# TensorE's program begins with leaps to two of its later points, and its loop is no longer put on a block edge

## The chip, the cores and the metric

The kernel runs on one core of a Trainium2 chip. A core has five engines with programs of their own (TensorE or PE, VectorE or DVE, ScalarE or ACT, GpSimd or POOL, SyncE or SP), which meet only at semaphores, and 16 DMA engines that carry data between main memory (HBM) and the on-chip memory, and the engines' own program code as well. The metric is device time in microseconds (us): lower is better.

## The reference

A decoding step for two batch entries (B = 2, one new position, D = 576) mixes an attention block with a dense block, by a gate:

```python
g = sigmoid((x * gate_w).sum(-1, keepdims=True))
q = (x @ wq).reshape(B, 1, H, Dh)            # H = 32 heads of Dh = 128
p = softmax(einsum("bhqd,bhkd->bhqk", q, k_cache) * Dh**-0.5)
a = einsum("bhqk,bhkd->bhqd", p, v_cache).reshape(B, 1, H * Dh) @ wo
b = gelu(x @ w1 + b1) @ w2 + b2              # F = 4608
return g * a + (1 - g) * b
```

All is float32. `k_cache` and `v_cache` have 4096 positions for each of 64 (batch, head) pairs, 134 MB each; the weights `wq`, `wo`, `w1`, `w2` are some 10 MB each. Everything is read once.

## The kernel before

**Data.** One large on-chip tile, `ring`, has three slots. `wq` and `w1` fill it first. The 64 heads are then taken in N = 16 quads of four (`E = 4`): quad i's K goes into slot i % 2, its V into slot 2 (the last V into slot 0). `w2` and `wo` follow into slots that come free. All large loads are issued by SyncE, in program order, so each waits there until its slot is released; the small ones (`b1`, the two rows of `x`, `gate_w`, `b2`) are issued by ScalarE.

**Before the quads.** TensorE's first work is `turn_x` (L318), which turns `x` and `gate_w` and needs the small loads; then come the gate, the projection with `wq`, the gathering of q, and the projection with `w1`. The first K load is issued when TensorE has read `wq`, the second when it has read `w1` (`load_k`, L474).

**A quad.** `scores(i)` (L517) multiplies K by q on VectorE and adds up over Dh, in part on GpSimd. `max_t` (TensorE) and `max_n` (VectorE) find the maximum, `softmax` (ScalarE) makes p. `attend` (L558) is 32 f32 matrix products on TensorE, p times V. `keep` (VectorE) and `combine` (TensorE) add the result to the accumulator.

**After the quads.** TensorE multiplies the 36 rows of `w2` into an accumulator (`acc_mm`), then rows 0 to 22 of `wo` (`FOLD = 23`). Rows 23 to 31 are done in four column parts each (`part`, L699), the last row's parts as their data lands; two copies and a store of 4.5 KB end the kernel.

**How the order is written.** The engines' programs are not in the order of the Python text but in lists: every call of `pe`, `dve`, ... appends an `Op` with its engine and what it reads and writes; `Flow.plan` works out the waits, and `Flow.write` (L91) writes each engine's list out. Operations marked `loop=(name, turn, place, slot)` are written once, as the body of a hardware loop (`nc.Fori`) with one register for the turn, whose waits are computed from the register. Only TensorE has such a loop: 15 turns of `attend`, `max_t`, `combine`. The last entry of the mark, 0, goes to `head_slot`: the loop's first instruction is loaded at slot 0 of a code block, the unit in which an engine's program is fetched, and a branch jumps over the padding ahead of it.

Of the kernel before, what the change touches and what calls it, by code (L numbers as in the profile page):

```python
# [27 lines left out]
class Flow:  # L28
# [12 lines left out]
    def op(self, engine, fn, r=(), w=(), a=(), dma=None, loop=None):  # L41
# [18 lines left out]
        self.ops.append(o)  # L60
        return o

    def plan(self):
        for o in self.ops:
            for d in o.deps:
                d.needed = True
        turns = {}
        for o in self.ops:
            if o.loop:
                turns.setdefault((o.loop[0], o.loop[2]), []).append(o)  # L70
        for same in turns.values():
            if any(o.needed for o in same):
                for o in same:
                    o.needed = True
        count, known = {}, {e: {} for e in ENGINES}
        for o in self.ops:
            k = known[o.engine]
            for d in sorted(o.deps, key=lambda d: -d.number):
                sem, v = d.done
                if k.get(sem, 0) < v:  # L80
                    o.waits[sem] = max(o.waits.get(sem, 0), v)
                    for s, n in d.knows.items():
                        k[s] = max(k.get(s, 0), n)
            sem = o.dma or o.engine
            count[sem] = count.get(sem, 0) + (16 if o.dma else 1 if o.needed else 0)
            o.done = sem, count[sem]
            o.knows = {**k, sem: max(k.get(sem, 0), count[sem])}
        self.count = count
        return turns

    def write(self):  # L91
        nc, turns = self.nc, self.plan()
        sems = {s: self.issued.get(s) or nc.alloc_semaphore(f"s_{s}") for s in self.count}
        for e in ("sp", "act", "pool", "dve", "pe"):
            at = self.at[e]
            ops = [o for o in self.ops if o.engine == e and o.dma not in self.issued]
            while ops:
                if not ops[0].loop:
                    self.emit(at, sems, ops.pop(0), None)
                    continue  # L100
                name, slot = ops[0].loop[0], ops[0].loop[3]
                body = [turns[k] for k in sorted(k for k in turns if k[0] == name)]
                assert ops[:len(body)] == [same[0] for same in body]
                ops = [o for o in ops if not o.loop or o.loop[0] != name]
                n = len(body[0])
                with nc.Fori(0, n, 1, engines=[at.engine], head_slot={at.engine: slot}) as i:
                    for same in body:
                        step = {}
                        for sem in {s for o in same[1:] for s in o.waits}:
                            v = [o.waits[sem] for o in same[1:]]  # L110
                            by = v[1] - v[0]
                            assert all(z - y == by for y, z in zip(v, v[1:])) and v[0] - by > 0
                            assert same[0].waits.get(sem, 0) <= v[0] - by
                            step[sem] = v[0] - by, by
                        assert set(same[0].waits) <= set(step)
                        self.emit(at, sems, same[0], (i, step))
        return sems

    def emit(self, at, sems, o, turn):
        if turn:  # L120
            for s, (base, by) in sorted(turn[1].items()):
                at.wait_ge(sems[s], turn[0] * by + base)
        else:
            for s, v in sorted(o.waits.items()):
                at.wait_ge(sems[s], v)
        i = o.fn()
        if o.dma:
            i.then_inc(sems[o.dma], 16)
        elif o.needed:
            i.then_inc(sems[o.engine], 1)  # L130
# [3 lines left out]
def kernel(  # L134
# [14 lines left out]
    nc = tc.nc  # L149
# [81 lines left out]
    with tc.tile_critical() as section:  # L231
        f = Flow(nc, {"first": first})
# [10 lines left out]
        def pe(fn, r=(), w=(), a=(), loop=None):  # L243
            return f.op("pe", fn, r, w, a, loop=loop)
# [9 lines left out]
        def mm(o, lhsT, rhs, start, stop):  # L254
            return ten.matmul(o, lhsT, rhs, start=start, stop=stop, skip_group_check=True)  # L255


        at = 0
        wts = {}
        for name, w in (("wq", wq), ("w1", w1)):  # L260
            n = w.shape[1]
# [162 lines left out]
        def half_mm(lhsT, rhs, k, s, start=False):  # L424
            o = 64 * (k % 2) + 32 * s
            return mm(acc[o:o + lhsT.shape[-1]], lhsT, rhs, start, False)

        def acc_mm(lhsT, rhs, k, start=False):
            for s in range(NS):
                i = half_mm(lhsT, rhs[:, s * DS:(s + 1) * DS], k, s, start)  # L430
            return i
# [32 lines left out]
        def slot(k):  # L464
            return ring[:, k * SLOT:(k + 1) * SLOT]
# [5 lines left out]
        def rows_of(t):  # L471
            return t.rearrange("p (r d) -> p r d", d=DH)
# [59 lines left out]
        def max_t(i, loop=None):  # L532
            pe(lambda: mm(mt, mxt.to_broadcast([P, P]), ident, True, True), r=["mxt", "ident"], w=["bank2"], loop=loop)

        def max_n(i):
            s = i % 2
            dve(
                lambda: vec.tensor_reduce(bs[s], mt.rearrange("o (e p) -> o e p", e=E), AX.X, ALU.max, negate=True),  # L538
                r=["bank2"], w=[f"bs{s}"],
            )  # L540

        def softmax(i):
            s = i % 2
            p = p_all[:, :NT * EB].rearrange("p (t c) -> p t c", c=EB)

            def fn():
                for e in range(E):
                    w = slice(e * PE_, (e + 1) * PE_)
                    ins = sca.activation(  # L549
                        p[w, :, e * RB:(e + 1) * RB], st[s][w].rearrange("p (t c) -> p t c", c=RB), AF.Exp,  # L550
                        bias=bs[s][w, e:e + 1], accum_out=rs[w, i * E + e:i * E + e + 1],
                    )
                return ins

            act(fn, r=[f"st{s}", f"bs{s}"], w=["p"], a=["rs"])
            act(lambda: sca.copy(now, pick[:, NO - E - i * E:2 * NO - E - i * E]), r=["pick"], w=["now"])

        def attend(i, name, loop=None):  # L558
            v = rows_of(slot(2 if name == "slot2" else 0))

            def fn():
                for t in range(NT):
                    j = t % 4
                    ins = mm(
                        av[32 * j:32 * j + 32], p_all[:, EB * t:EB * t + 32],
                        v[:, RB * t:RB * (t + 1)].rearrange("p r d -> p (r d)"), t < 4, t >= NT - 4,
                    )
                return ins

            pe(fn, r=["p", name], w=["bank4"], loop=loop)  # L570
# [8 lines left out]
        def combine(i, loop=None):  # L579
            pe(  # L580
                lambda: mm(oall, now, avs.rearrange("p r d -> p (r d)"), False, False),
                r=["now", "avs"], a=["bank1"], loop=loop,
            )

        for i in range(N):
            k = i - 1
            if i:
                max_n(k)
                softmax(k)
            scores(i)  # L590
            if i:
                attend(k, "slot2", loop=("quads", k, 0, 0))
                load_v(i)
            if i + 2 < N:
                load_k(i + 2)
            s = i % 2
            dve(lambda s=s: vec.tensor_reduce(mxt, st[s], AX.X, ALU.max), r=[f"st{s}"], w=["mxt"])  # L597
            max_t(i, loop=("quads", k, 1, 0) if i else None)
            if i:
                keep(k)  # L600
                combine(k, loop=("quads", k, 2, 0))


        srcs = {"w2": w2.rearrange("(p r) n -> p (r n)", r=NF), "wo": wo.rearrange("(p r) n -> p (r n)", r=32)}
# [12 lines left out]
        k = N - 1  # L617
# [8 lines left out]
        o = load_rows(2 * SLOT, "w2", 0, 14)  # L626
        o = load_rows(o, "w2", 14, 28)
        release(1)
        o = load_rows(SLOT, "w2", 28, NF)
        o = load_rows(o, "wo", 0, 9)  # L630
        o = load_rows(o, "wo", 9, 16)
# [3 lines left out]
        o = 0  # L635
        for a, z in ((16, 23), (23, 27), (27, 30), (30, 31)):
            o = load_rows(o, "wo", a, z)
        for a, z in ((0, DS), (DS, DS + DO), (DS + DO, D)):
            o = load_rows(o, "wo", 31, 32, (31 * D + a, 31 * D + z))
# [15 lines left out]
        turn = late(P)  # L655
# [18 lines left out]
        ops = bank[6][:, :NO]  # L674
# [13 lines left out]
        for r in range(NF):  # L688
            t, name = row("w2", r)
            pe(lambda t=t, r=r: acc_mm(hg[:, r], t, r), r=["hg", name], a=["bank0"])  # L690
        for r in range(FOLD):
            t, name = row("wo", r)
            pe(lambda t=t, r=r: acc_mm(oP[:, :, r], t, r), r=["oP", name], a=["bank0"])
# [34 lines left out]
        sems = f.write()  # L728
# [33 lines left out]
```

## Time and profile before

| | |
|---|---|
| median of 3 runs | 720.75 us (720.68 to 720.82) |
| profiled execution, time | 720.49 us |
| profiled execution, span from first to last instruction | 718.7 us |
| mean granted TensorE clock | 0.656 |
| busy: PE / DVE / ACT / POOL | 239.1 / 518.2 / 41.6 / 144.2 us |
| DMA | 308.71 MB, mean 430 GB/s |

The time of a run takes in a little before the first and after the last instruction, so the profiled execution's own time is 1.8 us more than its span. Times in the profile's rows count from the span's start. "Busy" is time in which an engine executed something; an idle engine matters only if it is what the end waits for. Queue q1 is SyncE's data queue, q10 ScalarE's; "instruction" queues carry program code.

### The profile page before, as it was taken

The page shows a single profiled execution, that of the slowest core. Times are in us where ns is not written, and L with a number is a line of the kernel's source. Part 1 is how long each engine was busy: PE and PEld are TensorE (multiplying, and loading weights), DVE is VectorE, ACT ScalarE, POOL GpSimd, SP SyncE. Part 2 cuts the span into 40 slices and gives each one's busy share as a digit, 9 for nine tenths or more (in the row PEclk, how much of TensorE's full clock was granted, in tenths as well). Part 3 has the DMA queues.
Part 4 walks back from the last instruction along what each step waited for, and adds up shares of the span by engine and source line. Part 5 has one row for each costly group of instructions (what it writes and reads, how often), then busy time and mean ns, then how long its engine had stood idle before and what let it go on. Part 6 is the DMA issues. An engine that isn't in the chain of part 4 may idle for free.

```text
span 718.7 us, 3903 instructions
## 1 busy us (share of the span) xinstructions
PE 239.1 (33%) x1659; PEld 68.5 (10%) x1659; DVE 518.2 (72%) x150; ACT 41.6 (6%) x157; POOL 144.2 (20%) x28
## 2 busy tenths in 40 slices
PE   0684004151514033140505060504123140506566
PEld 0221001010101000010101010101000010101122
DVE  0103999999969696969697896969696969698100
ACT  0020010101010101010101000010101010101000
POOL 1020133140404040311304040404040221304000
PEclk9977557565656657565757565666656575756788
DMA  9999999999999999999999999999999999999997
GB/s 411 409 428 450 419 453 419 445 430 430 434 427 445 423 445 430 434 441 423 438 423 452 423 441 434 430 441 419 445 423 449 427 441 434 427 441 423 420 428 322
DMA packets 7076, 308.71 MB, mean 430 GB/s; under 512 B 782, under 2 KB 1166, under 8 KB 1436
## 3 DMA queue, kind: packets, MB, share of 16 engines
q1 hardware_dynamic: 7044, 308.55, 99.3%
q8 instruction: 6, 0.10, 0.0%
q10 hardware_dynamic: 24, 0.05, 0.0%
q14 instruction: 2, 0.02, 0.0%
HBM read 308.59 MB, written 0.00 MB: 429 GB/s over the span
## 4 chain that ended last, share of the span: by engine, by line
DMA 56%; DVE 38%; PE 4%; POOL 0%; issue 0%; ACTq 0%; ACT 0%; POOLq 0%; DVEq 0%
DMA ring<-in_A_k_cache_dram 43%; DVE ring L521 22%; DVE st L526 11%; DMA ring<-in_A_v_cache_dram 6%; DVE st L528 5%; DMA ring<-in_A_wo_dram 4%; PE bank L255 4%; DMA ring<-in_gate_w_dram 3%; POOL ring L275 0%; PE bank L320 0%; DVE mxt L597 0%; DVE bs L538 0%; ACTq L250 0%; POOL ring L369 0%; DVE ring L313 0%
## 5 line engine op out<-in xcount | busy, mean ns | idle before, releaser
L521 DVE TENSOR_TENSOR ring<-ring,q_all 128x16384 f32<-128x16384 f32 x16 | 275.6, 17224 | 85.0 <-DMA ring<-in_A_k_cache_dram 85.0
L255 PE MATMUL bank<-ring,p_all 128*32 128x512 f32 x1024 | 146.5, 736 | 343.6 <-DMA ring<-in_A_v_cache_dram 343.6
L525 POOL TENSOR_TENSOR ring<-ring 128x3968 f32<-128x3968 f32 x16 | 138.0, 8624 | 473.1 <-DVE ring L521 473.1
L526 DVE TENSOR_REDUCE st<-ring 128x66 f32<-128x8448 f32 x16 | 143.2, 8953 | 0.6
L255 PEld LDWEIGHTS bank<-ring,p_all 128*32 128x32 f32 x1024 | 35.9, 132 | 458.9 <-DMA ring<-in_A_v_cache_dram 355.9
L528 DVE TENSOR_REDUCE st<-ring 128x62 f32<-128x3968 f32 x16 | 68.6, 4286 | 0.6
L549 ACT ACTIVATE p_all<-st,bs 32x128 f32<-32x128 f32 x64 | 25.5, 398 | 561.3 <-DVE bs L538 560.7
L255 PE MATMUL bank<-ring 128*32 128x384 f32 (+8 forms) x410 | 48.0, 526 | 11.2 <-DMA ring<-in_A_wo_dram 7.5
L255 PE MATMUL bank<-ident,mxt 128*128 128x128 f32 x32 | 9.2, 376 | 92.5 <-DVE mxt L597 92.5
L491 DVE TENSOR_TENSOR ring<-bank,ring 128x384 f32<-128x384 f32 x3 | 1.5, 553 | 32.6 <-PE bank L255 32.6
L724 DVE COPY ring<-bank 2x144 f32<-2x144 f32 x2 | 0.6, 300 | 33.3 <-PE bank L255 33.2
L255 PE MATMUL bank<-avs,now 128*64 128x512 f32 x32 | 23.5, 826 | 2.1 <-DVE avs L574 0.9
L574 DVE TENSOR_TENSOR avs<-bank,selr 128x512 f32<-128x512 f32 x16 | 10.9, 681 | 15.7 <-PE bank L255 15.7
L255 PEld LDWEIGHTS bank<-ring 128*32 128x32 f32 (+5 forms) x410 | 17.9, 122 | 40.8 <-issue 24.7
L255 PEld LDWEIGHTS bank<-ident,mxt 128*128 128x128 f32 x32 | 5.6, 220 | 106.8 <-DVE mxt L597 106.8
L313 DVE COPY ring<-ring 3x64 f32<-3x64 f32 x2 | 0.3, 181 | 19.4 <-DMA ring<-in_gate_w_dram 19.4
L255 PE MATMUL bank<-ring,hg 128*2 128x288 f32 x144 | 11.0, 462 | 2.6 <-DMA ring<-in_B_w_dram 2.6
L549 ACT ACTIVATION_READ_ACCUMULATOR p_all<-st,bs 32x1 f32 x64 | 11.8, 184 | 0.0
L408 POOL TENSOR_TENSOR ring<-ring 64x512 f32<-64x512 f32 x4 | 4.0, 1038 | 37.5 <-ACT ring L386 37.5
L320 PE MATMUL bank<-ident,ring 3*128 3x3 f32 x6 | 0.8, 254 | 23.8 <-DVE ring L313 23.8
L538 DVE TENSOR_REDUCE bs<-bank 128x4 f32<-128x128 f32 x16 | 4.7, 291 | 1.9 <-PE bank L255 1.9
L597 DVE TENSOR_REDUCE mxt<-st 128x1 f32<-128x128 f32 x16 | 4.6, 286 | 0.6
(65 smaller groups left out, 33.8 us busy)
## 6 DMA issues: line engine op xcount, KB each, us to landing
ring<-in_B_w_dram SPq DMA_DIRECT2D x1, 9216.0 KB, 46.2
ring<-in_B_w_dram SPq DMA_DIRECT2D x2, 4032.0 KB, 23.9
ring<-in_A_wo_dram SPq DMA_DIRECT2D x2, 2016.0 KB, 37.3
ring<-in_A_wo_dram SPq DMA_DIRECT2D x1, 2592.0 KB, 38.6
ring<-in_B_w_dram SPq DMA_DIRECT2D x1, 2304.0 KB, 32.8
ring<-in_B_w_dram SPq DMA_DIRECT2D x1, 1152.0 KB, 48.4
ring<-in_A_wo_dram SPq DMA_DIRECT2D x1, 1152.0 KB, 34.1
ring<-in_A_wq_dram SPq DMA_DIRECT2D x1, 1024.0 KB, 24.3
```

Of the source, the lines that this page charges most:

```text
L255: return ten.matmul(o, lhsT, rhs, start=start, stop=stop, skip_group_check=True)
L320: i = ten.transpose(xps[:, c, :B + 1], s, ident[:B + 1, :B + 1])
L408: lambda t=t, u=u: gps.tensor_mul(t, qall.unsqueeze(1).to_broadcast([NO, NQ, DH]), mine[:, u:u + NQ].unsqueeze(2).to_broadcast([NO, NQ, DH ...
L491: lambda m=m, b=b: vec.tensor_add(hrow[:, m * FC:(m + 1) * FC], bank[b][:, :FC], b1r[:, m * FC:(m + 1) * FC]), r=[f"bank{b}", "b1r"], a=[" ...
L521: lambda: vec.tensor_mul(kt, kt, q.unsqueeze(1).to_broadcast([P, R, DH])),
L525: pool(lambda: gps.tensor_add(h[:, :, :DH2], h[:, :, :DH2], h[:, :, DH2:]), r=[name], a=[name + "h"])
L526: dve(lambda: vec.tensor_reduce(st[s][:, HALVED:], kt[:, HALVED:], AX.X, ALU.add), r=[name], w=[f"st{s}"])
L528: lambda: vec.tensor_reduce(st[s][:, :HALVED], h[:, :, :DH2], AX.X, ALU.add),
L538: lambda: vec.tensor_reduce(bs[s], mt.rearrange("o (e p) -> o e p", e=E), AX.X, ALU.max, negate=True),
L549: ins = sca.activation(p[w, :, e * RB:(e + 1) * RB], st[s][w].rearrange("p (t c) -> p t c", c=RB), AF.Exp, bias=bs[s][w, e:e + 1], accum_o ...
L574: lambda: vec.tensor_mul(avs, av.rearrange("p (r d) -> p r d", d=DH), selr.unsqueeze(2).to_broadcast([P, RB, DH])), r=["bank4", "selr"], w ...
L597: dve(lambda s=s: vec.tensor_reduce(mxt, st[s], AX.X, ALU.max), r=[f"st{s}"], w=["mxt"])
```

## The change

`Flow` gets a method `stone`, which appends an operation without a function: a mark in an engine's list. TensorE's list gets two such marks: one ahead of its part of the first quad (ahead of `max_t(0)` and of the loop), and one behind the `w2` rows, ahead of the `wo` rows. Where an engine has marks, `write` now begins its program with a loop of two passes. In the first, with the register `turn` at 0, the compare-and-branch at each mark skips the work in front of the next one: the program branches to the first mark, from there to the second, sets `turn` to 1 and goes back to the start. In the second pass the work between the marks is done in order. What comes after the second mark follows the loop. The inner loop of 15 turns is no longer given a slot of a code block: it is loaded where it falls. The writing of one operation or loop moves into a method of its own, `next`, unchanged but for `head_slot`. The other engines' programs have no marks and stay as they are.

```diff
+    def stone(self, engine):
+        self.op(engine, None)
...
             ops = [o for o in self.ops if o.engine == e and o.dma not in self.issued]
+            stones = sum(o.fn is None for o in ops)
+            if stones:
+                turn = nc.alloc_registers(f"{e}_turn", engines=[at.engine])
+                nc.regs_mov(turn, 0)
+                with nc.Fori(0, 2, 1, engines=[at.engine]):
+                    for k in range(stones):
+                        work, stone = f"{e}_work{k}", f"{e}_stone{k}"
+                        nc.br_cmp(turn, 1, on_true=work, on_false=stone, comp_op="IS_EQ", engines=[at.engine])
+                        with nc.body(work, valid_engines=[at.engine]):
+                            while ops[0].fn:
+                                self.next(at, sems, ops, turns)
+                            ops.pop(0)
+                            nc.br(stone, engines=[at.engine])
+                        nc.switch_body(stone, valid_engines=[at.engine])
+                    nc.regs_mov(turn, 1)
             while ops:
...
+                self.next(at, sems, ops, turns)
         return sems
+
+    def next(self, at, sems, ops, turns):
...
-                with nc.Fori(0, n, 1, engines=[at.engine], head_slot={at.engine: slot}) as i:
+        with nc.Fori(0, n, 1, engines=[at.engine]) as i:
...
         for i in range(N):
             k = i - 1
+            if i == 0:
+                f.stone("pe")
             if i:
                 max_n(k)
                 softmax(k)
             scores(i)
             if i:
-                attend(k, "slot2", loop=("quads", k, 0, 0))
+                attend(k, "slot2", loop=("quads", k, 0))
...
             pe(lambda t=t, r=r: acc_mm(hg[:, r], t, r), r=["hg", name], a=["bank0"])
+        f.stone("pe")
         for r in range(FOLD):
             t, name = row("wo", r)
```

More of the change, by code (lines that the diff above doesn't have):

```diff
@@ L96, in write @@
             ops = [o for o in self.ops if o.engine == e and o.dma not in self.issued]
-            while ops:
[L98 to L105, printed above, removed]
-                with nc.Fori(0, n, 1, engines=[at.engine], head_slot={at.engine: slot}) as i:
[L107 to L116, printed above, removed]
@@ new lines, in write @@
+            while ops:
+                self.next(at, sems, ops, turns)
+        return sems
+    def next(self, at, sems, ops, turns):
+        nc = self.nc
+        if not ops[0].loop:
+            self.emit(at, sems, ops.pop(0), None)
+            return
+        name = ops[0].loop[0]
+        body = [turns[k] for k in sorted(k for k in turns if k[0] == name)]
+        assert ops[:len(body)] == [same[0] for same in body]
+        ops[:] = [o for o in ops if not o.loop or o.loop[0] != name]
+        n = len(body[0])
+        with nc.Fori(0, n, 1, engines=[at.engine]) as i:
+            for same in body:
+                step = {}
+                for sem in {s for o in same[1:] for s in o.waits}:
+                    v = [o.waits[sem] for o in same[1:]]
+                    by = v[1] - v[0]
+                    assert all(z - y == by for y, z in zip(v, v[1:])) and v[0] - by > 0
+                    assert same[0].waits.get(sem, 0) <= v[0] - by
+                    step[sem] = v[0] - by, by
+                assert set(same[0].waits) <= set(step)
+                self.emit(at, sems, same[0], (i, step))
@@ L597 @@
             dve(lambda s=s: vec.tensor_reduce(mxt, st[s], AX.X, ALU.max), r=[f"st{s}"], w=["mxt"])
-            max_t(i, loop=("quads", k, 1, 0) if i else None)
+            max_t(i, loop=("quads", k, 1) if i else None)
             if i:
                 keep(k)
-                combine(k, loop=("quads", k, 2, 0))
+                combine(k, loop=("quads", k, 2))
         srcs = {"w2": w2.rearrange("(p r) n -> p (r n)", r=NF), "wo": wo.rearrange("(p r) n -> p (r n)", r=32)}
```

## The prediction

> **What bounds the kernel now.** I read the page's DMA rows first, because the GB/s row of the slices is flat.
>
> ```profile
> span 718.7 us, 3903 instructions
> ...
> PE 239.1 (33%) x1659; PEld 68.5 (10%) x1659; DVE 518.2 (72%) x150; ACT 41.6 (6%) x157; POOL 144.2 (20%) x28
> ...
> q1 hardware_dynamic: 7044, 308.55, 99.3%
> q8 instruction: 6, 0.10, 0.0%
> ...
> q14 instruction: 2, 0.02, 0.0%
> ```
>
> TensorE is busy a third of the span, VectorE 72%; the 16 DMA engines carry ring traffic for 99.3%. The span is bytes over rate, plus a short end. The same rows hold what the change is about: queue q8 moved six packets of code, 0.10 MB, so 16 KB each. Asked window by window, the DMA view shows where they lie, 37:39, 60.5:62.5, 106.5:108.5, 676.5:678.5, 693:695 and 712.9:714.9, and one each; the first and last are shown, and between them the stretch 110:670, with no q8 row at all.
>
> ```profile
> q1 hardware_dynamic: 23, 0.85, 99.8%
> q8 instruction: 1, 0.02, 3.0%
> ...
> q1 hardware_dynamic: 4187, 242.73, 100.0%
> q14 instruction: 2, 0.02, 0.0%
> ...
> q1 hardware_dynamic: 461, 0.57, 79.2%
> q8 instruction: 1, 0.02, 3.0%
> ```
>
> A share of 3.0% of 16 engines over 2 us is 0.03 x 16 x 2 = 0.96 us of one engine: that is what one block of code costs the transfers. None is fetched in 110:670, where the loop turns. After the loop there are three. TensorE executes 2 x 1659 = 3318 matrix instructions; by the code 504 lie ahead of the loop (each f32 product is two weight loads and two matmuls) and a turn has 136, 2040 in 15 turns, which leaves 774 behind it. 774 over three fetches is one per 258: code is fetched block by block, as the program advances. So q8 is TensorE's.
>
> Next, does TensorE ever stand still for code? The chain of waits, first the start and then the end:
>
> ```profile
> 1.48 1.06 POOL ring L275
> ...
> 4.29 18.98 DMA ring<-in_gate_w_dram
> ...
> 23.80 0.86 PE bank L320 x6
> ...
> 24.99 10.94 PE bank L255 x74
> ...
> 35.94 34.24 DMA ring<-in_A_k_cache_dram
> ...
> 622.34 46.68 DMA ring<-in_A_v_cache_dram
> ...
> 669.15 8.58 PE bank L255 x64
> ...
> 677.75 31.71 DMA ring<-in_A_wo_dram
> ...
> 709.51 6.76 PE bank L255 x106
> ...
> 716.29 0.27 ACT ring L724
> ```
>
> Up to 23.80 TensorE waits for `gate_w`, the last of four small loads on ScalarE's queue. At the end it starts on wo rows 16 and up at 709.51. The 6.76 us that follow look like TensorE's, but the timeline's weight loads say that it catches up with the last rows as they land:
>
> ```profile
> 713.14 0.83 PEld L255 LDWEIGHTS bank<-ring 128*2 128x2 f32 x26 [0.34 <-issue]
> ...
> 715.21 0.11 PEld L255 LDWEIGHTS bank<-ring 128*2 128x2 f32 x8 [0.26 <-DMA ring<-in_A_wo_dram]
> 715.47 0.46 PEld L255 LDWEIGHTS bank<-ring 128*2 128x2 f32 x8 [0.15 <-DMA ring<-in_A_wo_dram]
> ```
>
> The last parts of row 31 wait for DMA (0.26, then 0.15 us). Around the fetch near 713.2 the idle ahead of the weight loads is 0.34 us, the beat of the rows before it: TensorE was not stopped by code there. So what ends the kernel is the last landing, plus one matmul, a copy and the store.
>
> **The change part by part.** (1) The walk. TensorE sets a register, enters a loop of two passes, and on the first pass branches to the first stone (ahead of the first `max_t`), from there to the second (behind the w2 rows), and back; on the second pass it works. A handful of register and branch instructions, at tenths of a us, before 23.80. The real price is that each leap lands in code not fetched yet. The trace has no missed branch, so I bound it. Below: 0.96 us, the packet alone. Above: 18.98 us, `gate_w` from issue to landing. Nearest to a block asked for while the engines are full of 64 KB rows is a step of ScalarE's queue:
>
> ```profile
> 2.57 1.10 ACTq L250 DMA_DIRECT2D ring<-in_B_b_dram  x1
> ...
> 4.29 0.29 ACTq L250 DMA_DIRECT2D ring<-in_gate_w_dram  x1
> ...
> 23.46 0.29 DVE L313 COPY ring<-ring 3x64 f32<-3x64 f32 x2 [19.36 <-DMA ring<-in_gate_w_dram]
> ```
>
> Four loads from 2.57 to 23.27 (4.29 + 18.98) are 5.2 us each; I take that. Two misses from about 1.5 us, where the engines begin (the chain's first row), end at 11.9, three (if the way back misses too) at 17.1. Both are before 23.80, so the cost on the path is 0. With the upper bound two misses would end at 39.5, 15.7 us late. How much lateness is free?
>
> ```profile
> 35.94 25.05 SPq L250 DMA_DIRECT2D ring<-in_A_k_cache_dram  x2
> ...
> 49.12 0.28 PEld L255 LDWEIGHTS bank<-ring 1*64 1x64 f32 x2 [0.92 <-issue]
> ...
> 51.02 0.20 PEld L255 LDWEIGHTS bank<-ring 128*32 128x32 f32 x8 [1.61 <-issue]
> ```
>
> SyncE issues the first K load at 35.94, when TensorE is done with wq, and the second at about 60.7 (the row's end, 35.94 + 25.05, less the 0.3 of one issue), when it is done with w1. The first K load lands at 35.94 + 34.24 = 70.18, so the second is queued 9.5 us before the engines need it; allow 2 for its start. TensorE also waits 1.61 us for w1's last rows at 51.02. So some 9 us of lateness, to 33, cost nothing; DMA runs dry only beyond that. The first K load has more room (it queues behind w1, whose rows are still arriving near 51).
>
> (2) Which fetches remain. If the blocks stay where they are put, each leap brings its target, and if the next block comes along as it does in straight running, four blocks arrive before 23.80; the straight run then asks for one more or none. Four or five fetches for six: the padding that put the loop on a block is gone too. The engines are full everywhere, so a fetch moved to the start costs its engine the same 0.96 us there. What counts is which of the 16 finishes last:
>
> ```profile
> 714.00:714.10 0.10, 0.10 (x12) 0.09 (x2) 0.00 (x0) 0.00 (x0) 0.00 (x0) 1.00 0.81 282
> ...
> 714.60:714.70 0.10, 0.10 (x14) 0.10 (x6) 0.00 (x0) 0.00 (x0) 0.00 (x0) 1.00 0.54 173
> ...
> 715.00:715.10 0.10, 0.10 (x10) 0.00 (x0) 0.00 (x0) 0.00 (x0) 0.00 (x0) 1.00 0.48 150
> ...
> 715.20:715.30 0.10, 0.10 (x8) 0.10 (x8) 0.00 (x0) 0.00 (x0) 0.00 (x0) 1.00 0.28 86
> ...
> 715.40:715.50 0.10, 0.10 (x10) 0.03 (x4) 0.00 (x0) 0.00 (x0) 0.00 (x0) 1.00 0.01 0
> ```
>
> The next to last column is the share of DMA engines busy. They drain over 1.5 us: 0.48 x 16, about eight, are still at work at 715.05, four or five at 715.25, none at 715.45. Three fetches fall behind 670, so at most three of these eight are late for that; if all three were freed, others would end at about 715.25. Gain 0.1 to 0.2 us; I take 0.15. Bounds: were every late engine brought to the middle of the drain (714.65) it would be 0.8 us; and if two of the early fetches meet on one of the late engines, it ends 0.96 us later than now.
>
> (3) The loop not aligned. 504 instructions and some ten waits and branches precede it; by 258 to a block, its 143 (136 and seven of waits and counting) begin near the start of the third block, shifted by whatever is loaded ahead of it, which the trace doesn't show. It lies inside a block unless that is over some 100 slots. Inside, or with both blocks kept, a turn costs as now: 0. In each turn TensorE waits for V, by the page's costliest matmul group, so tenths of a us more per turn are covered:
>
> ```profile
> L255 PE MATMUL bank<-ring,p_all 128*32 128x512 f32 x1024 | 146.5, 736 | 343.6 <-DMA ring<-in_A_v_cache_dram 343.6
> ```
>
> 343.6 us of idle over 16 turns is 21 us a turn.
>
> (4) Stone two behind the w2 rows: a branch, a move, an add and a compare ahead of wo row 0. TensorE waits there for data: 0.
>
> Sum against the profiled execution, 720.49 (span 718.7 and 1.8 around it): 0 + 0 + 0 + 0 - 0.15 = 720.35. The median of the runs is 720.75, 0.26 above that execution, so 720.6.
>
> [...]
>
> **The rivals.** *1, slower: blocks are not kept, and the loop straddles an edge.* Then the walk is lost (its fetches are repeated in the straight run), and each of 14 ways back finds its first block replaced by the one prefetched behind the loop. Two to three fetches a turn are 28 to 42 x 0.96 = 27 to 40 us of engine time, 1.7 to 2.5 us on each of 16: 722.4 to 723.3. It decides from two fetches a turn. For it: nothing shows a second block kept. Against: 143 instructions straddle only with a long preamble; I give the straddle one in four, two blocks one in three. Blocks not kept but no straddle: about 11 fetches in place of six, spread on more engines, 720.5 to 721.3, no change by the bound. Chance of rival 1: 0.08, with a walk so long that DMA runs dry (39.5 - 33 = 6.5 us, 727) in another 0.01.
>
> *2, faster: code fetches cost more than I see.* If the wait at 709.51 were late through q8 and not through wo's own bytes, and the drain were even, the gain would be the 0.8 us of the upper bound plus 0.96 of the fetch near 713.2, 1.7 us: 719.0. Against it: the ring is at 100.0% without any q8 in 110:670, and one fetch holds one engine in 16. 0.03.
>
> *3, the change does not do what it says:* the way back drops what was fetched, the six fetches come again where they were. Then the walk's fetches lie beside them: 720.7 to 721.2; its chance, 0.2, is part of "no change".
>
> **How the numbers follow.** Main case 0.68 (720.6; own range 720.3 to 721.2), rival 3 and its kin 0.2, rival 1 0.09, rival 2 0.03. Differences under 0.2% (1.44 us) are what I call the same: 0.88. Slower 0.09, faster 0.03. The range runs from half of the 0.8 us bound, 720.2, to a doubly charged late engine and a little of rival 1, 721.7.
>
> **What would show it.** Right: q8 packets before 24 us, four or so, and at most one behind 670; `gate_w` and first matmul still near 23.8; K loads issued near 35.9 and 60.7; none in 110:670; last landing of wo within 0.3 us of now. Wrong: q8 packets in the loop (rival 1), first matmul beyond 33, idle of "issue" ahead of TensorE in the last 10 us.

## The result, and the profile after

The changed kernel takes 723.42 us (median of 7 runs, 722.46 to 723.58), the kernel before 720.64 us in runs beside them: a ratio of 1.0035 (95% interval 1.0025 to 1.0044), 2.8 us slower. The seven runs lie in two clumps, three near 722.5 and four near 723.5. No change was forecast (720.6, range 720.2 to 721.7).

The page, and then the DMA view of the windows 0:20, 20:30, 110:670, 670:700 and 700:722 (the code queue's rows; for 110:670 all rows):

```profile
span 721.8 us, 3914 instructions
...
q1 hardware_dynamic: 7044, 308.55, 98.9%
q8 instruction: 10, 0.16, 0.1%
...
q8 instruction: 3, 0.05, 1.6%
...
q8 instruction: 2, 0.03, 1.9%
...
q1 hardware_dynamic: 4184, 242.80, 100.0%
q14 instruction: 2, 0.02, 0.0%
...
q8 instruction: 2, 0.03, 0.4%
...
q8 instruction: 1, 0.02, 0.3%
```

Ten blocks of code instead of six: five ahead of 30 us, two more by 110, none while the loop turns, and three behind it. The leaps brought five, and the straight run fetched its five all the same. The chain of waits, the start and the end:

```profile
4.28 18.99 DMA ring<-in_gate_w_dram
...
23.80 0.86 PE bank L344 x6
...
37.31 34.66 DMA ring<-in_A_k_cache_dram
...
680.05 32.58 DMA ring<-in_A_wo_dram
...
712.67 6.71 PE bank L279 x106
...
719.41 0.28 ACT ring L751
```

TensorE starts at 23.80, as before. The first K load, whose start moved (37.31 for 35.94) but which waits behind `w1` in either kernel, lands at 71.97 instead of 70.18: 1.8 us of the loss is there in the first 72 us. At the end wo rows 16 and up are in at 712.63 instead of 709.46. What the DMA engines do in the last microseconds, from the windows view (the next to last column is the share of the 16 engines at work; 0.06 is one of them):

```profile
715.00:715.10 0.10, 0.10 (x8) 0.07 (x2) 0.00 (x0) 0.00 (x0) 0.00 (x0) 0.50 0.46 167
716.00:716.10 0.10, 0.10 (x6) 0.03 (x2) 0.00 (x0) 0.00 (x0) 0.00 (x0) 1.00 0.33 127
717.00:717.10 0.10, 0.10 (x12) 0.08 (x8) 0.00 (x0) 0.00 (x0) 0.00 (x0) 1.00 0.06 23
718.00:718.10 0.10, 0.10 (x13) 0.05 (x4) 0.00 (x0) 0.00 (x0) 0.00 (x0) 1.00 0.06 23
718.40:718.50 0.10, 0.10 (x8) 0.00 (x0) 0.00 (x0) 0.00 (x0) 0.00 (x0) 1.00 0.07 23
```

Before, none was at work at 715.45. Now one engine alone, with fifteen idle, works on from 717 to past 718.4. The kernel waits for it. The totals hide this: bytes, rate and the busy times of the engines are nearly as before (308.78 MB at 428 GB/s, TensorE busy for 238.8 us, VectorE for 518.2).

### The profile page after: what moved, and what is told of

It is laid out like the page before. It is cut to its first block, busy times and chain, and to the rows that moved or that the text cites. A ratio compares the mean times of both kernels' runs of the same rounds, so it can differ in the third digit from the quotient of the medians.

```text
span 721.8 us, 3914 instructions
## 1 busy us (share of the span) xinstructions
PE 238.8 (33%) x1659; PEld 68.4 (9%) x1659; DVE 518.2 (72%) x150; ACT 41.6 (6%) x157; POOL 144.2 (20%) x28
## 2 busy tenths in 40 slices
DMA packets 7080, 308.78 MB, mean 428 GB/s; under 512 B 782, under 2 KB 1166, under 8 KB 1436
## 3 DMA queue, kind: packets, MB, share of 16 engines
q1 hardware_dynamic: 7044, 308.55, 98.9%
## 4 chain that ended last, share of the span: by engine, by line
DMA 56%; DVE 38%; PE 4%; POOL 0%; issue 0%; ACTq 0%; ACT 0%; POOLq 0%; DVEq 0%
DMA ring<-in_A_k_cache_dram 43%; DVE ring L545 21%; DVE st L550 11%; DMA ring<-in_A_v_cache_dram 6%; DVE st L552 5%; DMA ring<-in_A_wo_dram 5%; PE bank L279 4%; DMA ring<-in_gate_w_dram 3%; POOL ring L299 0%; PE bank L344 0%; DVE mxt L623 0%; DVE bs L562 0%; ACTq L274 0%; POOL ring L393 0%; DVE ring L337 0%
## 5 line engine op out<-in xcount | busy, mean ns | idle before, releaser
L279 PEld LDWEIGHTS bank<-ring 128*32 128x32 f32 (+5 forms) x410 | 17.6, 121 | 41.6 <-issue 21.8
```

## The experiments

Two theories were put to the test. *Pile*: the leaps' fetches come on top of the straight run's; each holds one DMA engine (for 0.96 us, by its packet), which would never catch up if each large load, which lands in 16 parts, gave every engine a fixed share; the end would be set by the engine that got most. *Layout*: the shifted blocks, or the loop that is not on a block edge, cost it.

**Leaps and layout apart.** Both marks removed, the loop still unaligned:

```diff
-            if i == 0:
-                f.stone("pe")
...
-        f.stone("pe")
```

> The changed kernel without its two marks: no leaps, only the loop left where it falls. Pile theory (the leaps' own fetches come on top of the six of the straight run, and the DMA engine that got most of them ends last): q8 has 5 packets, last wo landing within 0.3 us of the kernel before, 720.3 to 720.9. Rival, layout (the shifted blocks move the straight run's fetches onto engines that are late, or the loop pays for its place): 722.4 to 723.6 as with the change.

The leaps with the loop back on slot 0:

```diff
-        with nc.Fori(0, n, 1, engines=[at.engine]) as i:
+        with nc.Fori(0, n, 1, engines=[at.engine], head_slot={at.engine: 0}) as i:
```

> The leaps with the loop put back on slot 0 of a block. Pile theory: still about ten to eleven q8 packets, five of them before 24 us, and 722.3 to 724. Layout rival: back to 720.3 to 720.9.

The two marks moved into the first block (and taken out where they were):

```diff
         pe(turn_x, r=["xg", "xe", "ident"], w=["bank2"])
+        f.stone("pe")
...
         pe(gate, r=["gT", "xT"], w=["bank7"])
+        f.stone("pe")
```

> The same two marks, but the first behind turn_x and the second behind the gate product, some 30 instructions into the program: the walk stays in the first block and fetches nothing. Pile theory: 5 q8 packets, both leaps under 0.5 us, 720.3 to 720.9. Rival (the two-pass loop and its branches cost something by themselves): over 721.5.

Measured: without leaps 720.47 us (ratio 1.0000, 0.9991 to 1.0009; five q8 packets); aligned leaps 723.65 (1.0044, 1.0030 to 1.0057; eleven packets); near leaps 720.49 (0.9999, 0.9990 to 1.0008; five packets). The code queue's rows, without leaps and with aligned leaps:

```profile
q8 instruction: 5, 0.08, 0.0%
```

```profile
q8 instruction: 11, 0.18, 0.1%
```

The layout theory falls: the unaligned loop costs nothing (720.47), and saves a fetch that nobody misses (five packets for six, ten for eleven). The two-pass loop and its branches cost nothing either (720.49). The line view of the compare-and-branch shows the leaps, of the near ones and then of the changed kernel (durations in ns: least, median, longest):

```profile
L109 PEldq COMPARE_BRANCH  x4: 71/138/217, 1.7 to 23.8; - x4
```

```profile
L109 PEldq COMPARE_BRANCH  x4: 71/4132/9097, 1.7 to 59.5; - x4
```

In the trace the two far leaps take 8.2 and 9.1 us, the near ones 0.2: TensorE stands at the branch until a block is in (the packet of the first leap's fetch ends at 8.5 us, the leap at 9.9). The walk, way back included, ends at 19.8 us, ahead of 23.80.

**One leap instead of two.** Only the first mark, or only the second (the other `f.stone("pe")` removed).

> Only the first mark (ahead of max_t(0)): one leap out and back. Pile theory: two or three fetches before 24 us, of which two coincide, then the straight run's five; the latest DMA engine ends some 3 us behind the first at the first K load (3.5 with the change, 1.7 before), and 721.8 to 723.3. If the cost grew evenly with the number of extra fetches, three of five would give 722.3; if it takes both leaps to make a pair of fetches at once, 720.6 to 721.5.

> Only the second mark (behind the w2 rows): one leap out and back, further. [...]

Measured: 721.98 (1.0020, 1.0011 to 1.0029) and 721.92 (1.0020, 1.0010 to 1.0029). Half the loss each, at either distance; but the halves do not add up leap by leap, as the section on the sum below shows. Three fetches come early in each: one near 7.6 and two at once near 15.

**The pair.** Two fetches at once looked worse than one: by the trace's packets a fetch alone takes 0.9 to 1.1 us, one of a pair 1.5 to 2.2, and the 64 KB packet of data that its engine moves next (taken to be the one that starts as the fetch ends) is often longer too, 2.9 us behind a single and up to 3.7 behind a pair (3.60 in the changed kernel), for 2.42 elsewhere (the kernel before shows the single's too: 2.97 behind the fetch at 61.0). To part them, an empty loop at each mark:

```diff
                         nc.switch_body(stone, valid_engines=[at.engine])
+                        with nc.Fori(0, 15, 1, engines=[at.engine]):
+                            at.nop()
```

with the first mark only, and with both:

> Only the first mark, and at the mark an empty loop of 15 turns (some 6 us by the 0.4 us of a loop's way back) before the way back, so that the block fetched behind the target and the one fetched after the return are not asked for at the same moment. Pair theory: three single fetches of some 1 us, no pair of 1.5 and 2.2 us; the latest engine about 1.7 us behind the first at the first K load, and 720.4 to 721.2. Count theory (it is the three extra fetches, wherever they fall): 721.8 to 722.2, as without the dwell. The same empty loop is passed again later, where TensorE waits for the scores: no cost there.

> Both marks, with the empty loop at each. Five fetches one by one; the walk ends near 31 us, under the 33 us up to which lateness is free. Pair theory: 720.5 to 721.5. Count theory: 722.4 to 723.6, as with the change.

The DMA view, window 14:17.5, one leap without and then with the dwell:

```profile
q8 instruction: 2, 0.03, 6.6%
```

```profile
q8 instruction: 1, 0.02, 1.9%
```

6.6% of 16 engines over 3.5 us is 3.7 us for two packets, 1.9% is 1.06 us for one. The first K load, without and with:

```profile
36.84 35.08 DMA ring<-in_A_k_cache_dram
```

```profile
36.95 33.34 DMA ring<-in_A_k_cache_dram
```

It lands at 71.92 and at 70.29. Time with the dwell: 720.49 (0.9999, 0.9990 to 1.0008), with the same eight fetches as without. So three extra fetches are free where they come one at a time, and cost 1.5 us where two coincide. The trace does not name the engine of a fetch, so the dwell may also have moved the fetches to other engines. But in all six profiled kernels in which the leap or leaps make a pair near 15 us and the loads start in time, the first K load, which lands in 16 parts (taken to be one for each DMA engine, since a share of 0.06, one engine, is at work while one part is out), has 3.3 to 3.5 us from its first part to its last, and in both with the dwell 1.9.

With both marks it was a miss in part: 722.02 (1.0020, 1.0011 to 1.0029; single runs 721.42 to 722.88), where the pair theory said 720.5 to 721.5. That profile has no pair, and the first K load lands at 70.48 as it should; but of the straight run's fetches the one near 675 sets a part of the loads from 1.4 to 2.9 us behind the first, and the one near 694 sets another, late already, from 2.2 to 3.8. (The one near 711 falls on an engine that is not late.) The last load's 16 parts land 3.6 us apart. Ten fetches on 16 engines can meet. Some 0.5 us of that profile's loss is not in this spread: TensorE starts at 28.91, 5.1 us late, and the first part of the second K load lands 0.6 us later than before (88.40 for 87.79).

**One engine loaded with data.** No code at all: ScalarE stores a partition row of `q_all` to main memory eight or sixteen times, behind q's last copy:

```diff
+        scr = nc.dram_tensor("scr", [8, N * DH], F32, kind="Internal").ap()
+        for j in range(8):
+            load(scr[j:j + 1], q_all[0:1].rearrange("p u d -> p (u d)"), r=[f"q{g}" for g in range(N // NQ)],
+                 w=[f"scr{j}"], e="act", key="scr")
...
```

One more line makes the sixth K load wait for the stores, which are done long before it is issued.

> The kernel before, with eight stores of one partition row of q_all (8 KB, one packet each by the row loads of this size, about 0.31 us) to a scratch buffer, issued by ScalarE at about 48 us. No code is fetched for it. If they all fall on one DMA engine (2.5 us together) and the end is set by the latest engine: 721.3 to 723. If they are spread over the engines: 720.4 to 720.9.

> Sixteen such stores, 5 us together. On one engine: another 2.5 us above eight, 723.8 to 725.5. Spread: 720.5 to 721.1.

Measured: 721.99 (1.0020, 1.0011 to 1.0029) and 724.66 (1.0057, 1.0043 to 1.0071). The DMA issues and the end of the kernel with sixteen:

```profile
scr<-q_all ACTq DMA_DIRECT2D x16, 8.0 KB
```

```profile
718.00:718.10 0.10, 0.10 (x14) 0.10 (x8) 0.00 (x0) 0.00 (x0) 0.00 (x0) 1.00 0.06 23
718.60:718.70 0.10, 0.10 (x10) 0.08 (x4) 0.00 (x0) 0.00 (x0) 0.00 (x0) 1.00 0.06 23
719.20:719.30 0.10, 0.10 (x12) 0.09 (x8) 0.00 (x0) 0.00 (x0) 0.00 (x0) 1.00 0.07 23
719.60:719.70 0.10, 0.10 (x8) 0.02 (x4) 0.00 (x0) 0.00 (x0) 0.00 (x0) 1.00 0.01 0
```

128 KB, stored before 125 us, are 0.04% of the bytes and cost 4.1 us, 600 us later, on one engine: of the last load's 16 parts one lands 5.7 us behind the first and the next latest 1.7, as before. This is the pile, with plain data. Eight more stores cost 2.7 us, about eight packets of 0.3 us. The contrast is a row of K copied within main memory, behind the first K load, once or twice:

```diff
+        scr = nc.dram_tensor("scr", [1, SLOT], F32, kind="Internal").ap()
+        for j in range(1):
+            load(scr[j:j + 1], k_cache[1, 31].rearrange("(p r) d -> p (r d)", r=R)[j:j + 1], w=[f"scr{j}"])
```

> The kernel before, with one more row of K (64 KB) copied to a scratch buffer in main memory behind the first K load; no leaps. If the end is set by the one DMA engine that has most to do, a row that falls whole on one engine (2.42 us by the K packets) delays it: 720.5 plus 0.7 to 2.4, so 721.2 to 723. If work is shared out among the engines, 64 KB is 0.15 us: 720.4 to 720.9.

> Two such rows. If both fall on the same engine, another 2.4 us above the kernel with one row: 723.6 to 725.5. On two engines: as with one row. Shared out: 0.3 us, 720.6 to 721.

Measured: 720.63 (1.0003, 0.9994 to 1.0012) and 720.88 (1.0005, 0.9996 to 1.0014). The trace has 16 packets of 4 KB for each row: shared out, as the second branch of the expectation had it, and as cheap.

**Does a block stay?** The walk made twice:

```diff
-                with nc.Fori(0, 2, 1, engines=[at.engine]):
+                with nc.Fori(0, 3, 1, engines=[at.engine]):
...
-                        nc.br_cmp(turn, 1, ...
+                        nc.br_cmp(turn, 2, ...
...
-                    nc.regs_mov(turn, 1)
+                    nc.regs_alu(turn, turn, 1, op=ALU.add)
```

> Three passes in place of two: the walk is made twice before the work. If blocks that were fetched are kept, the second walk's leaps take about 0.4 us each, as the way back did (0.43), the second walk fetches nothing new, first matmul stays at 23.8 us, and the time is that of the change, 722.4 to 723.6. If they are not kept, the second walk takes another 17 us and fetches four or five more blocks: 15 q8 packets, first matmul at about 38 to 42 us, later than the 33 us from which the transfers run dry, and 726 to 735.

Measured: 733.84 us (1.0184, 1.0166 to 1.0202). The second walk's leaps take 12.6 and 8.4 us: what the first had fetched did not spare them. But of the straight run's five fetches only one was left. That was left open by the theory, so three more, one of them a second profile:

> Only the first mark, walked to twice. If a second walk makes the blocks stay (as the kernel that walks twice to both marks showed only one q8 packet after 50 us, near 721), the straight run fetches fewer than its five. If that was particular to its late start, five again. Time: the second leap ends near 20 us if it misses as long as the first, so the first matmul stays near 24: 721 to 723, by whether its fetches coincide.

> Only the second mark, walked to twice. The same question; if the blocks around the second mark stay, no q8 packet near 694 and 710, none of the last loads is disturbed, but the early fetches still leave one engine late: 721.5 to 723. If not, packets near 675, 694 and 710 as ever.

> The kernel that walks twice to both marks, a second profile: if the blocks do stay, again nine q8 packets up to 50 us and one near the end; if the first profile had lost records, about fourteen.

The second profile of both marks walked to twice, windows 0:30, 30:50, 50:700 and 700:731:

```profile
q8 instruction: 5, 0.08, 1.8%
...
q8 instruction: 4, 0.07, 1.8%
...
q1 hardware_dynamic: 4981, 277.75, 98.8%
q14 instruction: 2, 0.02, 0.0%
...
q8 instruction: 1, 0.02, 0.2%
```

The same again (732.68 in its one run). With the first mark twice (721.98; 1.0020, 1.0011 to 1.0029) the straight run lacks its fetches near 38 and 62 and has those near 675, 694 and 710. With the second mark twice (723.37; 1.0038, 1.0024 to 1.0052) it has all five. So after a second walk some blocks are not fetched again (four of five with both marks, in two profiles, two with the first, none with the second), and the late start is not what does it: with the first mark twice TensorE starts at 24.99, only 1.2 us late, and two fetches are spared. What decides whether a block is found again stays open.

**One sum for all.** In the profiled executions of this table the time less the spread of the last load (from the first to the last of its parts) is nearly the same:

| kernel | q8 packets | spread of the last load, us | profiled time, us | difference |
|---|---|---|---|---|
| before | 6 | 1.69 | 720.49 | 718.8 |
| no leaps | 5 | 1.75 | 720.43 | 718.7 |
| near leaps | 5 | 1.60 | 720.28 | 718.7 |
| first mark with dwell | 8 | 1.93 | 720.55 | 718.6 |
| first mark | 8 | 3.30 | 722.04 | 718.7 |
| second mark | 8 | 3.43 | 721.79 | 718.4 |
| both with dwell | 10 | 3.62 | 722.88 | 719.3 |
| the change | 10 | 4.87 | 723.58 | 718.7 |
| the change, aligned | 11 | 4.86 | 723.65 | 718.8 |
| 8 stores | 6 | 3.26 | 722.10 | 718.8 |
| 16 stores | 6 | 5.73 | 724.79 | 719.1 |

The row copies and the kernels that walk twice to one mark give 718.6 to 718.9 as well. Only the kernel that walks twice to both marks stands apart (733.84 less 1.62 is 732.2): there the loads start late.

The spread, not the number of fetches, gives the time. In the changed kernel it is 3.5 us already at the first K load (1.7 before) and 3.4 near 700; the fetch near 710 then makes it 4.9. The landings show each fetch of the straight run behind the loop by itself: the one near 675 moves a part from 0.1 to 1.6 us behind the first, the one near 694 another from 1.7 to 3.2, and the one near 710 the latest, from 3.4 to 5.0, while the next latest stays at 3.2. So a single fetch costs its engine 1.5 us, and the kernel pays only where that engine is among the latest. This is where the loss of both leaps comes from, beyond that of one: the second leap's pair, near 22.3 and 23.0, leaves the spread at the first K load as one leap does, 3.5 and 3.3 to 3.4, and the rest is the fetch near 710. Why it fell on the latest engine is not shown (one late fetch does so with aligned leaps and with the second mark twice, none with one leap made once). That the runs near 722.5 are those where it did not is inferred from the size, 1 us, and not shown.

## Why the prediction was wrong

- *What bounds the kernel* held: the last landing (718.92) ends it, and TensorE was not stopped by code at the end (its last weight loads wait for wo at 718.55).
- *Step 1, the walk*, held in its sum (0 on the path, first matmul at 23.80) and missed the price of a leap: 8.2 and 9.1 us where 5.2 were taken, inside the bounds of 0.96 and 18.98. The way back found its block, in 0.43 us.
- The lateness that is free was put at 9 us, with an allowance of 2 us for a load's start (the first packets of the kernel before begin 1.0 us after the issue of the first load, 1.76 for 0.74). Walked twice, TensorE starts at 41.4, 17.6 late, and 13.3 us are lost, so at most 4.3 were free there. The sum missed that delayed K loads add up: the first is issued at 54.7 us, 18.8 late, and lands 6.4 late; the second waits for the same TensorE, is issued 19.0 late and lands 12.2 late.
- *Step 2, which fetches remain and what they cost, failed*, twice. "If the blocks stay where they are put" took four or five fetches, at most one of them late, and a gain of 0.15 us: ten came, three of them behind 670, since after a single walk the straight run fetches everything again. And the price of a fetch was taken as its packet, 0.96 us. With the stretched packet behind it a single costs its engine 1.5 us, and one of two at once some 3 (packets of 1.87 and 2.20 us near 15 us, and the data packets behind them 1.2 and 1.0 longer than 2.42). The upper bound allowed two fetches to meet on a late engine at 0.96; the last landing moved from 715.80 to 718.92, by a pair and then a single on engines that were late.
- *Step 3*, the loop not aligned: held, 0.
- *Step 4*: held, as the near leaps and the dwell confirm (branches and an empty loop where TensorE waits cost nothing: 720.49 us with either).
- *The rivals.* The third named the right event, the fetches repeated where they were, and put it at 720.7 to 721.2: a term mis-sized by more than 2 us, since it added the walk's fetches as if they spread out. The first was half right (blocks lost) and wrong where it took its price from (no fetch in the loop); that its 722.4 to 723.3 lies next to the measured 723.4 is chance. Its case without a straddle, "about 11 fetches in place of six, spread on more engines", is what happened, with ten, and it was priced at 720.5 to 721.3 by the same mistake as the third. The chance of the first rests on one in three for two blocks, the author's estimate: no run shows how many blocks are held. The runs showed leaps of 8.2 and 9.1 us, a straight run that fetches its five again after one walk, and one that fetches one to five of them after two.

The lesson in the working: the drain rows of the kernel before (0.48, then 0.28 of the engines still at work) showed engines that end 1.5 us apart: those that were free did not take over the work of the others. So a surplus on the latest engine is paid in full, and the range was still built as if extra fetches spread out.

## What to carry to other kernels

This kernel is bound by transfers (the data queue at 98.9% of 16 engines), and its time followed the latest of the 16 parts of the last load: time less spread is 718.4 to 719.3 us in the eleven profiles of the table. In a kernel like it, count what falls on one engine (here 1.5 us for a block of code, 0.3 for the 8 KB store of one row), not total bytes, and look at the share of engines at work in the last microseconds (0.06 from 717 to past 718.4). A fetch of code is traffic too: 16 KB, 0.9 to 1.1 us of one engine where it comes alone. Don't fetch ahead code that arrives in time anyway: the time without leaps (720.47) and with leaps that fetch nothing (720.49) is the time before (720.52 beside them), so there was no stall to remove, and this loop needs no alignment.

## What the runs showed of the hardware that was not expected

- A surplus on one DMA engine lasts: in the changed kernel the 16 parts of a load land 3.53 us apart at 52 us and 3.38 at 706, with eight stores 3.43 at 91 us and 3.26 at the end. It was seen to go only where the transfers ran dry (both marks walked to twice, the spread is 3.4 us at 52 us and 0.7 at the first K load, which is issued at 54.7).
- The 64 KB data packet that starts as a code fetch ends is longer than the usual 2.42 us: by 0.5 us behind a single one (2.92 behind the changed kernel's fetch at 7.55, 2.97 behind the fetch at 61.0 before) and by up to 1.3 behind one of two at once (3.60 and 3.42 behind the changed kernel's pair near 15 us). 16 KB of code, fetched beside another 16 KB, cost some 3 us of an engine (2.20 and 1.0 in that pair).
- A copy of 64 KB within main memory was shared out (16 packets of 4 KB), and eight stores of 8 KB from one partition row were not (one part of the last load late, a spread of 3.26 us): +0.1 us for the one (720.63 for 720.51), +1.4 us for the other (721.99 for 720.57).
- Which engine a fetch falls on, and why two at once are slower, stays open.
